# Attention and soft mixture of experts on one core: value rows in interleaved key order, a fourth value tile, and another opening

## The chip, the cores and the metric

The kernel runs on one core of a Trainium2 chip. The metric is device time in microseconds (us), the median of several runs. One more execution was profiled; everything below that is read from a trace comes from that execution.

## The reference

Queries attend in chunks of 32 to 8 memory keys, 16 keys to the left, the chunk's own 32 and 8 to the right (64 keys). The result x, 3072 rows of 512, goes through a soft mixture of eight experts.

```python
for c in range(nc):                      # 24 chunks of 32
    q_c = q[:, :, c_start:c_end]
    k_full = np.concatenate([mem_k, k[:, :, l_start:r_end]], axis=2)
    v_full = np.concatenate([mem_v, v[:, :, l_start:r_end]], axis=2)
    scores = scale * np.matmul(q_c, k_full.transpose(0, 1, 3, 2))
    a = softmax(scores)
    out[:, :, c_start:c_end] = np.matmul(a, v_full)
...
logits = x @ phi                         # 512 x 32
slot_input = softmax(logits, 0).T @ x    # 32 slots, 4 of each expert
h = np.maximum(slot_input[e] @ w1[e], 0.0); slot_out[e] = h @ w2[e]
return softmax(logits, 1) @ slot_out
```

## The kernel before

**Units.** The attention runs over 12 units (`NU`) of 256 queries, all 8 heads. In iteration i the loop turns the attention result of unit i-1 around (`transpose_x`), multiplies probabilities by values for unit i (`values`, tile `a`), makes scores for unit i+2 (`scores`, tile `s`) and transposes the probabilities of unit i+1 (`transpose_p`). VectorE subtracts the row maximum (`softmax`, tile `p`), ScalarE takes the exponent, VectorE sums and divides. After each pair of units the logits of the experts and a running `D` are brought up to date. Every engine keeps the order of the program text (`InOrder`); waits between engines come from the tiles' dependences.

**Tiles and loads.** All loads are issued on the sync engine's queue (SP), in program order, and a load waits there until its tile is free. Queries `q` (512 KB a unit) fill 128 partitions. Keys `k` come as two loads of 64 rows, for the two heads of a pair, onto every second partition. Values of a unit lie in two tiles: the even chunks' `e` and the odd chunks' `o`, each row 4 KB. `e` comes in two loads of 64 rows onto every second partition of 0 to 127 (from `vw`). The odd chunk's window shares its first 32 keys with the last 32 of `e`, so only 32 new rows a head are loaded (from `vx`), onto every second partition of 0 to 63, and `share_v` copies partitions 64 to 127 of `e` into `o` on GpSimd (POOL). `first_k` is a small POOL copy that puts the first chunk's keys beside the others; the scores wait for it. There are three buffers (`NB`) of `q`, `k` and of the value pair.

**Weights.** The expert weights are 64 pieces of 512 KB, 32 of `w1` and then 32 of `w2`. `load_w(upto)` issues pieces up to a count. The first 15 go to slabs of their own (`NW`); the count grows by 1.5 a unit (`WRATE`) through unit 7 and is then `usable[...]`, which adds the buffers of `k`, `q`, `v` and `x` as their last unit is done, 36 slabs in all. Later pieces take the slab of the piece 36 before. `hT` and other late tiles lie in a value pair that is no longer needed.

**Opening.** Tiles whose other head's half must be zero are cleared once: `k` by VectorE and POOL, the `e` tiles by ScalarE (three copies), the lower half of the `o` tiles by VectorE and POOL. Then follow the loads of units 0 to 2, with `first_k` and `share_v` between them in POOL's order.

After the attention the slot inputs are formed, four steps of two experts each run (tile `h`), then `w2` in two column blocks (tile `so`), each followed by `combine`, which writes half of the output.

Of the kernel before, what the change touches and what calls it, by code (L numbers as in the profile page):

```python
# [10 lines left out]
F32 = mybir.dt.float32  # L11
# [4 lines left out]
P = 128  # L16
# [27 lines left out]
NEG = -1.0e30  # L44
PIECE = 1024
NB = 3
NW = 15
W0 = 1
WRATE = 1.5
WLAST = 8  # L50
WARM0 = 8
WARM1 = 3
# [18 lines left out]
def tile_attn_softmoe(  # L71
# [2 lines left out]
    qT: bass.AP,  # L74
    kT: list,
    vw: bass.AP,
    vx: bass.AP,
    phi: bass.AP,
    w1: bass.AP,
    w2: bass.AP,  # L80
# [7 lines left out]

    q_t = [cp.tile([P, NPAIR, U], F32, tag=f"q{i}", name=f"q{i}") for i in range(NB)]
    k_t = [cp.tile([P, 2, KW], F32, tag=f"k{i}", name=f"k{i}") for i in range(NB)]  # L90
    v_t = [[cp.tile([P, 2, VW], F32, tag=f"v{i}{o}", name=f"v{i}{o}") for o in range(2)] for i in range(NB)]
    x_t = [cp.tile([P, 4, DM], F32, tag=f"x{i}", name=f"x{i}") for i in range(2)]
    w_slab = [cp.tile([P, PIECE], F32, tag=f"w{i}", name=f"w{i}") for i in range(NW)]
    lT = cp.tile([P, NG, P], F32, tag="lT", name="lT")
    late = [v_t[(NU - NB) % NB][o].rearrange("p a n -> p (a n)") for o in range(2)]
    hT = late[0].rearrange("p (e f s) -> p e f s", e=E, s=NSLOT)
    c_sb = late[1][:, 0:4 * NG * NSLOT].rearrange("p (u s) -> p u s", s=NSLOT)
    cst = [late[1][:, 4 * NG * NSLOT + P * G:4 * NG * NSLOT + P * G + P] for G in range(NG)]
# [16 lines left out]
    def load_q(u):  # L115
        sp.dma_start(q_t[u % NB], qT[u])
# [24 lines left out]
        pool.tensor_copy(out=kx[:, :, :, lo:CHUNK], in_=own[:, :, :, 0:CHUNK - lo])  # L141

    def load_v(u):
        e, o = v_t[u % NB]
        for h in range(2):
            sp.dma_start(e[h:P:2, h], vw[u, 64 * h:64 * h + 64])
        for h in range(2):
            sp.dma_start(o[h:P // 2:2, h], vx[u, CHUNK * h:CHUNK * h + CHUNK])

    def share_v(u):  # L150
        e, o = v_t[u % NB]
        pool.tensor_copy(out=o[P // 2:P], in_=e[P // 2:P])

    slabs = list(w_slab)
    freed = []
    for d in range(NB):
        u = NU - NB + d
        flat = k_t[u % NB].rearrange("p a n -> p (a n)")
        freed += [(2 * u - 3, flat[:, 0:PIECE]), (2 * u - 3, flat[:, PIECE:2 * PIECE])]
        freed += [(2 * u - 3, q_t[u % NB].rearrange("p g n -> p (g n)"))]  # L160
        if d:
            freed += [(2 * u, v_t[u % NB][o][:, a]) for o in range(2) for a in range(2)]
    flat_x = [t.rearrange("p u n -> p (u n)") for t in x_t]
    last = (NG - 1) % 2
    freed += [(2 * NU, flat_x[1 - last][:, 0:PIECE]), (2 * NU, flat_x[1 - last][:, PIECE:2 * PIECE])]
# [22 lines left out]
    pool.memset(k_t[0][:, 1], 0.0)  # L190
    make_identity(nc, ident)
    load_q(0)
    load_k(0)
    dve.memset(v_t[0][1][0:P // 2], 0.0)
    dve.memset(k_t[1][:, 0], 0.0)
    pool.memset(k_t[1][:, 1], 0.0)
    for u in range(NB):
        e = v_t[u][0].rearrange("p h n -> p (h n)")
        act.copy(out=e, in_=warm[:, 0:1].broadcast_to([P, 2 * VW]))
    load_k(1)  # L200
    load_q(1)
    load_v(0)
    first_k(0)
    dve.memset(v_t[1][1][0:P // 2], 0.0)
    share_v(0)
    load_v(1)
    sp.dma_start(phi_sb, phi.rearrange("(kc p) s -> p kc s", p=P))
    first_k(1)
    dve.memset(k_t[2][:, 0], 0.0)
    pool.memset(k_t[2][:, 1], 0.0)  # L210
    load_k(2)
    load_q(2)
    share_v(1)
    pool.memset(v_t[2][1][0:P // 2], 0.0)
    load_v(2)
    first_k(2)
    load_w(W0)
    w_ps = row(P, "warm_ps")

# [40 lines left out]
    def softmax(u, tiles):  # L260
        mx = wk.tile([P, 16, 1], F32, tag="mx", name=f"mx{u}")
        p = pexp[u] = wk.tile([P, 8, 4 * CHUNK], F32, tag="p", name=f"p{u}")
        step = NSUB // len(tiles)
        for a, t in enumerate(tiles):
            if u % UPB == 0 and a == 0:
                dve.memset(t[0:32, 0, :, :, 0:LEFT], NEG)
            if u % UPB == UPB - 1 and a == len(tiles) - 1:
                dve.memset(t[96:128, step - 1, :, :, CHUNK - RIGHT:CHUNK], NEG)
            m = mx[:, 8 * step * a:8 * step * (a + 1)]
            dve.tensor_reduce(out=m[:, :, 0], in_=t.rearrange("p s g h n -> p (s g h) n"), axis=AX.X, op=ALU.max)  # L270
            for h in range(2):
                dve.tensor_tensor(
                    out=p[:, 4 * step * a:4 * step * (a + 1)].rearrange("p m (n h) -> p h m n", h=2)[:, h],
                    in0=t.rearrange("p s g h n -> p h (s g) n")[:, h],
                    in1=m.rearrange("p (m h) o -> p h m o", h=2)[:, h].broadcast_to([P, 4 * step, 2 * CHUNK]),
                    op=ALU.subtract,
                )

# [25 lines left out]
    def values(u, pt):  # L304
        a_ps = banks(f"a{u}", "A").rearrange("p s (g h d) -> p s g h d", g=NPAIR, h=2)
        for s in range(NSUB):
            for g in range(NPAIR):
                for j in range(4):
                    v = v_t[u % NB][j % 2].rearrange("p h (i g d) -> p h i g d", g=NPAIR, d=D)
# [97 lines left out]
    for i in range(NU):  # L407
        G = (i - 2) // 2 if i >= 2 else None
        first = i % 2 == 0
        if i >= 1:  # L410
            transpose_x(i - 1)
        if i + 1 < NU:
            exponent(i + 1)
        if G is not None and not first:
            dispatch_t(G)
        a_ps = values(i, pt)
        if G is not None and first:
            l_ps = logits(G)
        if G is not None and not first:
            dispatch(G)  # L420
        normalize(i, a_ps)
        if i + 3 < NU:
            load_v(i + 3)
        load_w(W0 + int(WRATE * (i + 0.5)) if i < WLAST else usable[2 * i])
        if G is not None and first:
            dispatch_max(G, l_ps)
            dispatch_exp(G, l_ps)
        if G is not None and not first:
            dispatch_z(G)
            dispatch_sum(G)  # L430
# [184 lines left out]
def _layouts(inputs):  # L615
# [52 lines left out]
```

## Time and profile before

| | |
|---|---|
| median of 3 runs | 191.42 us (190.03 to 193.74) |
| the profiled execution | 187.95 us |
| its span, first to last instruction | 186.2 us |
| PE busy | 146.5 us (79%) |
| DVE busy | 101.2 us (54%) |
| ACT busy | 62.7 us (34%) |
| POOL busy | 36.3 us (19%) |
| bytes moved by DMA | 63.12 MB, mean 339 GB/s |

PE is TensorE, DVE VectorE, ACT ScalarE, POOL GpSimd, SP the sync engine whose queue issues the loads. Times in rows are in us from the start of the span. A share of busy time is an average over stages with different limits, so it names no bound by itself. The DMA share is the mean busy share of the core's 16 DMA engines; a transfer that takes longer than it should counts as busy too, so the share is read together with the GB/s beside it.

### The profile page before, as it was taken

The numbers are of one execution on the slowest core, as the hardware profiler recorded it, in microseconds if no ns is written. First come the engines' busy times: TensorE is split into PE (matmuls) and PEld (weight loads), VectorE is DVE, ScalarE is ACT, GpSimd is POOL, SyncE is SP. The second block draws the span as 40 slices with busy tenths as digits, with TensorE's granted clock in tenths as the row PEclk, the third lists the DMA queues.
The fourth block names the chain that finished last, engine by engine and source line by source line (L and its number), as shares of the span: only waits on it lengthen the run. The fifth ranks groups of instructions, "written<-read, shape, count | busy, mean of one in ns | idle before, by whom it ended". The sixth has DMA issues, their size and how long they took to land.

```text
span 186.2 us, 6128 instructions
## 1 busy us (share of the span) xinstructions
PE 146.5 (79%) x2649; PEld 108.2 (58%) x2649; DVE 101.2 (54%) x179; ACT 62.7 (34%) x122; POOL 36.3 (19%) x43
## 2 busy tenths in 40 slices
PE   4821996884999599789799588579999978867960
PEld 4711795773879488659778485264565635411530
DVE  6860399592679959597899934320560007100360
ACT  7620136231624806354273362200322006000350
POOL 6006901452223404050521800000000000000000
PEclk9996699999699999999999969957999999975576
DMA  5699789999999999999999999999999999999596
GB/s 164 217 276 219 229 258 383 340 392 284 386 293 314 323 338 383 260 362 258 334 303 263 388 402 415 410 407 408 408 410 406 409 406 408 408 411 420 213 407 249
DMA packets 18219, 63.12 MB, mean 339 GB/s; under 512 B 3088, under 2 KB 3088, under 8 KB 18192
## 3 DMA queue, kind: packets, MB, share of 16 engines
q1 hardware_dynamic: 18192, 62.73, 95.2%
q8 instruction: 21, 0.34, 0.8%
q14 instruction: 6, 0.05, 0.1%
HBM read 56.43 MB, written 6.29 MB: 337 GB/s over the span
## 4 chain that ended last, share of the span: by engine, by line
PE 46%; DMA 20%; DVE 16%; issue 7%; ACT 5%; SPq 1%; DVEq 0%; POOL 0%; ACTq 0%
PE s L65 10%; PE a L65 8%; PE h L65 7%; DMA w<-in_w_dram 5%; DMA k<-in_w_dram 5%; DMA v<-in_w_dram 5%; PE xt_ps L65 5%; PE pt_ps L65 4%; DMA v<-in_vw_dram 4%; DVE p L65 4%; DVE z L65 3%; DVE mx L65 3%; PE o L65 3%; ACT v L65 3%; DVE x L65 3%
## 5 line engine op out<-in xcount | busy, mean ns | idle before, releaser
L65 PE MATMUL s<-k,q 128*32 128x128 f32 x768 | 27.5, 292 | 13.9 <-POOL k L65 8.1
L65 PEld LDWEIGHTS s<-k,q 128*32 128x32 f32 x768 | 23.9, 118 | 18.3 <-issue 8.9
L65 POOL COPY v<-v 64x2048 f32<-64x2048 f32 x12 | 22.7, 1896 | 52.0 <-DMA v<-in_vw_dram 37.0
L65 PE MATMUL a<-v,pt 128*32 128x128 f32 x768 | 25.1, 277 | 4.6 <-issue 4.4
L65 ACT COPY pt<-pt_ps 128x512 f32<-128x512 f32 x24 | 13.1, 590 | 40.3 <-PE pt_ps L65 40.1
L65 PEld LDWEIGHTS a<-v,pt 128*32 128x32 f32 x768 | 20.8, 111 | 8.1 <-issue 6.4
L65 DVE TENSOR_REDUCE mx<-s 128x16 f32<-128x1024 f32 (+1 forms) x13 | 14.8, 1142 | 14.0 <-PE s L65 13.7
L65 DVE TENSOR_TENSOR x<-a,z 128x1024 f32<-128x1024 f32 x12 | 14.7, 1224 | 8.1 <-PE a L65 7.2
L65 PE MATMUL pt_ps<-ident,p 128*128 128x128 f32 x96 | 14.6, 298 | 2.5 <-issue 2.3
L65 DVE TENSOR_TENSOR p<-s,mx 128x512 f32<-128x512 f32 (+1 forms) x26 | 15.8, 656 | 0.5
L65 ACT ACTIVATE p<-p 128x1024 f32<-128x1024 f32 (+1 forms) x13 | 12.9, 994 | 7.0 <-DVE p L65 6.7
L65 PE MATMUL xt_ps<-ident,x 128*128 128x128 f32 x96 | 14.5, 298 | 0.9 <-DVE x L65 0.5
L65 ACT COPY xT<-xt_ps 128x512 f32<-128x512 f32 x24 | 13.4, 604 | 4.7 <-PE xt_ps L65 4.7
L65 DVE TENSOR_REDUCE z<-p 128x16 f32<-128x1024 f32 x12 | 14.6, 1214 | 0.0
L65 PEld LDWEIGHTS pt_ps<-ident,p 128*128 128x128 f32 x96 | 11.3, 150 | 5.2 <-issue 4.6
L65 PEld LDWEIGHTS xt_ps<-ident,x 128*128 128x128 f32 x96 | 12.4, 155 | 2.0 <-DVE x L65 1.4
L65 DVE COPY so_sb<-so 128x256 f32<-128x256 f32 x2 | 0.8, 424 | 19.7 <-PE so L65 19.7
L65 PE MATMUL o<-shl,v 32*128 32x256 f32 x96 | 9.8, 530 | 1.4 <-ACT shl L65 0.9
L65 PEld LDWEIGHTS o<-shl,v 32*128 32x128 f32 x96 | 6.5, 249 | 5.0 <-ACT shl L65 2.0
L65 POOL COPY k<-k 128x192 f32<-128x192 f32 (+2 forms) x20 | 5.8, 295 | 17.9 <-DMA k<-in_k_dram 17.2
L65 ACT COPY shl<-r 128x256 f32<-128x256 f32 x2 | 0.7, 373 | 23.5 <-PE r L65 23.5
L65 PE MATMUL h<-w,siT 128*32 128x256 f32 x120 | 8.5, 443 | 0.0
(95 smaller groups left out, 169.9 us busy)
## 6 DMA issues: line engine op xcount, KB each, us to landing
w<-in_w_dram SPq DMA_DIRECT2D x30, 512.0 KB, 9.8
q<-in_qT_dram SPq DMA_DIRECT2D x12, 512.0 KB, 7.2
v<-in_vw_dram SPq DMA_DIRECT2D x24, 256.0 KB, 7.9
k<-in_w_dram SPq DMA_DIRECT2D x12, 512.0 KB, 10.1
v<-in_w_dram SPq DMA_DIRECT2D x12, 512.0 KB, 10.2
v<-in_vx_dram SPq DMA_DIRECT2D x24, 128.0 KB, 7.6
q<-in_w_dram SPq DMA_DIRECT2D x6, 512.0 KB, 10.1
k<-in_k_dram SPq DMA_DIRECT2D x8, 296.0 KB, 7.0
```

The source lines that it names most:

```text
L65: return self.tc.keep_in_program_order(f(*args, **kwargs))
```

## The change

Positions in the score window are reordered. A probability column that stood for key 32b+j now lies at 2j+b, and the rows of the value tiles lie in the same order. In `o` the new rows then fall on every second row of a head, that is on partitions 4r and 4r+1 of all 128, and the shared rows on the others. `share_v` copies the whole of `e` into `o` (128 partitions), and `load_new` then overwrites the new rows from DRAM; it is issued at the top of iteration u-2 and waits for that copy. Units 0 and 1 load all 64 rows a head of `o` from DRAM instead (`load_odd`), with no copy. There is a fourth value pair (`NV`), so `e` is loaded four units ahead, not three; `NW` falls to 11 and `WRATE` to 1.25 to make room. The tiles cleared and the order of the opening differ. `phi` is laid out on the host so that each partition reads one run.

```diff
+NV = 4
+NDIRECT = 2
-NW = 15
+NW = 11
-WRATE = 1.5
+WRATE = 1.25
...
     def load_v(u):
-        e, o = v_t[u % NB]
+        e = v_t[u % NV][0]
         for h in range(2):
-            sp.dma_start(e[h:P:2, h], vw[u, 64 * h:64 * h + 64])
+            sp.dma_start(e[h:P:2, h], vw[u, 0, 64 * h:64 * h + 64])
+
+    def load_odd(u):
+        o = v_t[u % NV][1]
         for h in range(2):
-            sp.dma_start(o[h:P // 2:2, h], vx[u, CHUNK * h:CHUNK * h + CHUNK])
+            sp.dma_start(o[h:P:2, h], vw[u, 1, 64 * h:64 * h + 64])
 
     def share_v(u):
-        e, o = v_t[u % NB]
-        pool.tensor_copy(out=o[P // 2:P], in_=e[P // 2:P])
+        e, o = v_t[u % NV]
+        pool.tensor_copy(out=o, in_=e)
+
+    def load_new(u):
+        o = v_t[u % NV][1]
+        for h in range(2):
+            sp.dma_start(o[h:P:4, h], vw[u, 1, 64 * h:64 * h + 64:2])
...
-        if d:
-            freed += [(2 * u, v_t[u % NB][o][:, a]) for o in range(2) for a in range(2)]
+    for u in range(NU - NV + 1, NU):
+        freed += [(2 * u, v_t[u % NV][o][:, a]) for o in range(2) for a in range(2)]
...
+    dve.memset(warm, 0.0)
     dve.memset(k_t[0][:, 0], 0.0)
-    dve.memset(warm, 0.0)
     pool.memset(k_t[0][:, 1], 0.0)
+    for u in range(NDIRECT):
+        clear_v(act, u, 0)
+        clear_v(act, u, 1)
     make_identity(nc, ident)
+    dve.memset(k_t[1][:, 0], 0.0)
+    pool.memset(k_t[1][:, 1], 0.0)
     load_q(0)
     load_k(0)
-    dve.memset(v_t[0][1][0:P // 2], 0.0)
-    dve.memset(k_t[1][:, 0], 0.0)
-    pool.memset(k_t[1][:, 1], 0.0)
-    for u in range(NB):
-        e = v_t[u][0].rearrange("p h n -> p (h n)")
-        act.copy(out=e, in_=warm[:, 0:1].broadcast_to([P, 2 * VW]))
     load_k(1)
     load_q(1)
-    load_v(0)
-    first_k(0)
-    dve.memset(v_t[1][1][0:P // 2], 0.0)
-    share_v(0)
-    load_v(1)
-    sp.dma_start(phi_sb, phi.rearrange("(kc p) s -> p kc s", p=P))
-    first_k(1)
     dve.memset(k_t[2][:, 0], 0.0)
     pool.memset(k_t[2][:, 1], 0.0)
+    clear_v(dve, 2, 0)
+    first_k(0)
+    for u in range(NDIRECT):
+        load_v(u)
+        load_odd(u)
+    sp.dma_start(phi_sb, phi)
+    first_k(1)
+    clear_v(pool, 3, 0)
+    load_v(2)
     load_k(2)
     load_q(2)
-    share_v(1)
-    pool.memset(v_t[2][1][0:P // 2], 0.0)
-    load_v(2)
     first_k(2)
+    share_v(2)
+    load_v(3)
     load_w(W0)
...
                 dve.tensor_tensor(
-                    out=p[:, 4 * step * a:4 * step * (a + 1)].rearrange("p m (n h) -> p h m n", h=2)[:, h],
-                    in0=t.rearrange("p s g h n -> p h (s g) n")[:, h],
-                    in1=m.rearrange("p (m h) o -> p h m o", h=2)[:, h].broadcast_to([P, 4 * step, 2 * CHUNK]),
+                    out=p[:, 4 * step * a:4 * step * (a + 1)].rearrange("p m (j s h) -> p h m j s", s=2, h=2)[:, h],
+                    in0=t.rearrange("p s g h (b j) -> p h (s g) j b", b=2)[:, h],
+                    in1=m.rearrange("p (m h) o -> p h m o", h=2)[:, h].rearrange(
+                        "p m (o z) -> p m o z", z=1).broadcast_to([P, 4 * step, CHUNK, 2]),
                     op=ALU.subtract,
...
     for i in range(NU):
+        if NDIRECT <= i + 2 < NU:
+            load_new(i + 2)
...
         normalize(i, a_ps)
-        if i + 3 < NU:
-            load_v(i + 3)
+        if i + NV < NU:
+            load_v(i + NV)
...
         if i + 3 < NU:
             first_k(i + 3)
-        if i + 2 < NU:
-            share_v(i + 2)
+            share_v(i + 3)
```

## Rows read from the trace of the kernel before

**Rows 1.** Page, 40 slices of 4.66 us: DMA share in tenths, then GB/s.

```profile
DMA  5699789999999999999999999999999999999596
GB/s 164 217 276 219 229 258 383 340 392 284 386 293 314 323 338 383 260 362 258 334 303 263 388 402 415 410 407 408 408 410 406 409 406 408 408 411 420 213 407 249
```

**Rows 2.** Two stretches: length, busy per engine, granted clock, DMA share, GB/s.

```profile
8.00:109.00 101.00, 80.12 (x1835) 69.16 (x1828) 74.62 (x119) 38.87 (x74) 33.00 (x34) 0.94 0.99 315
109.00:170.40 61.40, 53.25 (x726) 29.96 (x724) 15.97 (x46) 12.98 (x34) 0.00 (x0) 0.89 1.03 410
```

**Rows 3.** The same view of short stretches inside the attention.

```profile
30.00:35.00 5.00, 2.90 (x96) 2.36 (x86) 3.01 (x5) 1.06 (x1) 2.78 (x4) 1.00 1.02 419
35.00:37.00 2.00, 2.00 (x27) 1.73 (x16) 1.58 (x3) 1.09 (x3) 0.00 (x0) 1.00 1.07 249
...
50.50:53.50 3.00, 3.00 (x91) 2.25 (x82) 1.82 (x2) 0.00 (x0) 0.00 (x0) 1.00 1.03 231
...
84.00:87.00 3.00, 3.00 (x67) 2.80 (x56) 1.66 (x4) 0.98 (x3) 0.00 (x0) 1.00 1.00 215
```

**Rows 4.** Timeline of SP's queue: start, time, tile and source of the issued loads.

```profile
2.25 4.76 SPq L65 DMA_DIRECT2D k<-in_k_dram  x4
...
7.69 1.11 SPq L65 DMA_DIRECT2D v<-in_vw_dram  x2
8.84 1.23 SPq L65 DMA_DIRECT2D v<-in_vx_dram  x2
...
15.35 4.20 SPq L65 DMA_DIRECT2D k<-in_k_dram  x2
...
31.13 1.14 SPq L65 DMA_DIRECT2D v<-in_vx_dram  x2
```

**Rows 5.** Page, DMA issues: source, count, KB each, median us to landing.

```profile
v<-in_vx_dram SPq DMA_DIRECT2D x24, 128.0 KB, 7.6
```

**Rows 6.** Chain that ended last, in order of time: start, time, what.

```profile
10.75 6.88 DMA v<-in_vw_dram
...
17.68 0.24 POOL k L65
...
160.40 9.99 DMA v<-in_w_dram
```

**Rows 7.** Timeline of PE's matmuls: start, time, tile, count, idle before and its releaser.

```profile
17.96 3.64 PE L65 MATMUL s<-k,q 128*32 128x128 f32 x64 [7.44 <-POOL k L65]
...
23.21 2.01 PE L65 MATMUL a<-v,pt 128*32 128x128 f32 x62 [0.24 <-DMA q<-in_qT_dram]
...
48.74 2.34 PE L65 MATMUL a<-v,pt 128*32 128x128 f32 x64
...
65.19 1.39 PE L65 MATMUL a<-v,pt 128*32 128x128 f32 x41 [1.97 <-issue]
...
111.00 1.96 PE L65 MATMUL a<-v,pt 128*32 128x128 f32 x64
...
124.86 1.51 PE L65 MATMUL h<-w,siT 128*32 128x256 f32 x12
```

**Rows 8.** Timeline of POOL, columns as in the group before.

```profile
15.43 1.89 POOL L65 COPY v<-v 64x2048 f32<-64x2048 f32 x1 [8.60 <-DMA v<-in_vw_dram]
...
21.05 1.80 POOL L65 MEMSET v<- 64x2048 f32 x1
...
105.04 1.83 POOL L65 MEMSET v<- 128x2048 f32 x1
```

**Rows 9.** Groups of instructions by line and shape: busy us, mean ns of one.

```profile
L65 DVE TENSOR_TENSOR p<-s,mx 128x512 f32<-128x512 f32 x22 | 14.3, 699 | 0.4
...
L65 ACT COPY v<-warm 128x2048 f32<-128x2048 f32 x3 | 5.5, 1894 | 0.4 <-DVE warm L65 0.4
...
L65 DVE TENSOR_REDUCE stats<-l 128x1 f32<-128x128 f32 x6 | 1.7, 283 | 2.2 <-PE l L65 2.2
...
L65 DVE TENSOR_REDUCE nms<-nm_ps 32x32 f32<-32x128 f32 x1 | 0.3, 278 | 1.0 <-PE nm_ps L65 1.0
```

More of the change, by code (lines that the diff above doesn't have):

```diff
@@ L76, in tile_attn_softmoe @@
     vw: bass.AP,
-    vx: bass.AP,
     phi: bass.AP,
@@ L90, in tile_attn_softmoe @@
     k_t = [cp.tile([P, 2, KW], F32, tag=f"k{i}", name=f"k{i}") for i in range(NB)]
-    v_t = [[cp.tile([P, 2, VW], F32, tag=f"v{i}{o}", name=f"v{i}{o}") for o in range(2)] for i in range(NB)]
+    v_t = [[cp.tile([P, 2, VW], F32, tag=f"v{i}{o}", name=f"v{i}{o}") for o in range(2)] for i in range(NV)]
     x_t = [cp.tile([P, 4, DM], F32, tag=f"x{i}", name=f"x{i}") for i in range(2)]
@@ L94, in tile_attn_softmoe @@
     lT = cp.tile([P, NG, P], F32, tag="lT", name="lT")
-    late = [v_t[(NU - NB) % NB][o].rearrange("p a n -> p (a n)") for o in range(2)]
+    late = [v_t[(NU - NV) % NV][o].rearrange("p a n -> p (a n)") for o in range(2)]
     hT = late[0].rearrange("p (e f s) -> p e f s", e=E, s=NSLOT)
@@ L184, in load_w, with clear_v @@
                 sp.dma_start(s, w2[at[0], at[1], :, at[2]])
+    def clear_v(eng, u, o):
+        t = v_t[u][o].rearrange("p h n -> p (h n)")
+        if eng is act:
+            act.copy(out=t, in_=warm[:, 0:1].broadcast_to([P, 2 * VW]))
+        else:
+            eng.memset(t, 0.0)
+    dve.memset(warm, 0.0)
     dve.memset(k_t[0][:, 0], 0.0)
-    dve.memset(warm, 0.0)
     pool.memset(k_t[0][:, 1], 0.0)
+    for u in range(NDIRECT):
+        clear_v(act, u, 0)
+        clear_v(act, u, 1)
     make_identity(nc, ident)
+    dve.memset(k_t[1][:, 0], 0.0)
+    pool.memset(k_t[1][:, 1], 0.0)
     load_q(0)
     load_k(0)
-    dve.memset(v_t[0][1][0:P // 2], 0.0)
-    dve.memset(k_t[1][:, 0], 0.0)
-    pool.memset(k_t[1][:, 1], 0.0)
-    for u in range(NB):
-        e = v_t[u][0].rearrange("p h n -> p (h n)")
-        act.copy(out=e, in_=warm[:, 0:1].broadcast_to([P, 2 * VW]))
     load_k(1)
     load_q(1)
-    load_v(0)
-    first_k(0)
-    dve.memset(v_t[1][1][0:P // 2], 0.0)
-    share_v(0)
-    load_v(1)
-    sp.dma_start(phi_sb, phi.rearrange("(kc p) s -> p kc s", p=P))
-    first_k(1)
     dve.memset(k_t[2][:, 0], 0.0)
     pool.memset(k_t[2][:, 1], 0.0)
+    clear_v(dve, 2, 0)
[7 more added lines that the diff above has]
+    load_v(2)
     load_k(2)
     load_q(2)
-    share_v(1)
-    pool.memset(v_t[2][1][0:P // 2], 0.0)
-    load_v(2)
     first_k(2)
+    share_v(2)
+    load_v(3)
     load_w(W0)
@@ L308, in values @@
                 for j in range(4):
-                    v = v_t[u % NB][j % 2].rearrange("p h (i g d) -> p h i g d", g=NPAIR, d=D)
+                    v = v_t[u % NV][j % 2].rearrange("p h (i g d) -> p h i g d", g=NPAIR, d=D)
                     pe.matmul(
@@ L443, in tile_attn_softmoe @@
         load_w(W0 + int(WRATE * (i + 1)) if i < WLAST else usable[2 * i + 1])
-        if i == NU - NB + 1:
+        if i == NU - NV + 1:
             pool.memset(hT, 0.0)
@@ L643, in windows @@
         return w.transpose(0, 4, 2, 3, 5, 1, 6).reshape(NU, 2 * len(first), CP, NPAIR * D)
-    vw = windows(range(2 * CHUNK))
-    vx = windows(range(2 * CHUNK, STEP + HALO))
+    even = [CHUNK * (r % 2) + r // 2 for r in range(2 * CHUNK)]
+    odd = [CHUNK * (2 - r % 2) + r // 2 for r in range(2 * CHUNK)]
+    vw = np.stack([windows(even), windows(odd)], axis=1)
+    phi = inputs["moe_phi"].reshape(NKC, P, NSLOT).transpose(1, 0, 2)
     w2 = inputs["moe_w2"].reshape(E, NFC, P, NBLK, WB).transpose(3, 0, 2, 1, 4).reshape(NBLK, E, P, 2, PIECE)
-    return {"qT": qT, **kT, "vw": vw, "vx": vx, "phi": inputs["moe_phi"], "w1": inputs["moe_w1"], "w2": w2}
+    return {"qT": qT, **kT, "vw": vw, "phi": phi, "w1": inputs["moe_w1"], "w2": w2}
 def kernel(**inputs):
```

## The prediction

> **What bounds the kernel now.** I read the slices first [rows 1]. From the third slice to the 37th the DMA engines are 70 to over 90% busy, yet until about 100 us the GB/s lie between 219 and 392, and after that near 408. Two stretches put that in one number each [rows 2]: from 8 to 109 us share 0.99 at 315 GB/s, from 109 to 170.4 us share 1.03 at 410. Engines that are always busy and carry a quarter less must be taking longer over each transfer. Short stretches show that this is no even slowness [rows 3]: 419 GB/s in one, then 249, 231 and 215, share at or above 1.00 throughout. The half-speed phases last 2 to 3 us and come once a unit, some 3 to 4 us after the two `vx` loads are issued (31.13 in [rows 4], phase from 35). Those are the only loads confined to partitions 0 to 63. Where only loads over all 128 partitions are in flight, such as `q`, `k` and `vw`, the rate is that of the weights. That `vx` slows everything beside it is my inference; the trace names no cause.
>
> The chain ends in weights, the last landing at 170.4 [rows 6]; 15.8 us of output follow. So to 170.4 the bound is DMA. Two side bounds matter if DMA gets cheaper. PE needs 62.3 us from `values(3)` to `values(11)`, 7.78 a unit, six gaps of "issue" among them (one is 1.97) [rows 7]. And `h` starts 13.9 us after `values(11)`.
>
> In the opening the second scores start at 17.96 after PE idled 7.44 [rows 7], released by `first_k(1)` [rows 6]. That copy stood in POOL's order behind `share_v(0)`, which itself waited 8.60 for `vw` [rows 8].
>
> **The change part by part.** *New rows on every fourth partition.* The bytes of `vx` stay (two loads of 32 rows a unit), but they spread over all 128 partitions. At 410 instead of 315 GB/s the 31.8 MB moved from 8 to 109 us would take 77.6 us: up to 23.4 us are to be had, at least nothing if the slowness comes with loads of 32 rows and not with their place. I take nearly all, since 64-row and 128-row loads, both spread, run at 398 to 419.
>
> [...]
>
> *Direct odd tiles.* Units 0 and 1 load 64 rows a head, not 32: four times 128 KB more, 0.52 MB, 1.3 us at 410 GB/s. A `vx` load takes 7.6 us to land [rows 5], so the new rows, issued about 1.5 units ahead, have some 4 us to spare. `phi` (64 KB, 0.2 us) is hidden behind the first units.
>
> *Opening.* `first_k(1)` no longer stands behind a value copy. `k` of unit 1 is issued by 7.0 us [rows 4]; with the 6.9 us to landing of a `vw` load under traffic [rows 6] it is there by 13.9, and the earliest is 10.5, when PE would otherwise idle. So the second scores gain 4.1 to 7.4 us. I take 6.7, nearer the upper end, because `k` goes ahead of the value loads on the queue: `values(0)` at 16.5 in place of 23.2 [rows 7]. ScalarE clears four tiles rather than three, 1.9 us more [rows 9], before it has an exponent to do; hidden, and at most 1.9 us otherwise. `k` of unit 2 now stands behind 2.6 MB of value rows rather than 1.6, but SP no longer waits until 15.35 to issue it.
>
> *Copies.* `share_v` writes 128 partitions in place of 64. A memset of 64 partitions takes 1.80, of 128 takes 1.83 [rows 8], so the copy stays at 1.89. There are 10, not 12. It moves one unit earlier, as does its `e`.
>
> *The wait of `load_new`.* At the top of iteration i SP waits for `share_v(i+2)`. Behind it stand `e` of unit i+4, weights and `k` and `q` of unit i+5. By my count `e` lands near the middle of iteration i-1 and the copy ends about when SP gets there: 0 to 3 us of wait. Transfers already issued cover it: a `vw` load takes 6.9 us from issue to landing. Cost nothing; 3 us for each of ten units where the cover fails.
>
> *`p` in the new order.* VectorE now reads PSUM alternately 32 elements apart. The nearest rows: a maximum over 128 PSUM elements taken 32 apart is 278 ns (`nms`), over 128 in a row 283 (`stats`) [rows 9]. So 699 ns a subtraction stays, two a unit. Bounds: nothing, or the double, 1.4 us a unit.
>
> *Fewer slabs.* By the end of unit 7 11 pieces may be out, not 13; in unit 8 14 and 17, not 18 and 21; from unit 9 on the counts agree (21, 24, 28, 32). All inputs and 11 pieces are 29.2 MB; 1.5 MB are moved by 8 us [rows 1], the rest takes 67.5 us: done at 75.5. If units take 7.6 us, `values(8)` ends near 79, so DMA idles up to 4 us there.
>
> **The sum.** Bound by DMA: 58.5 MB are moved by 170.4 now (1.5, 31.8 and 25.2 [rows 1, 2]), 59.0 after. From 8 us 57.5 MB at 410 take 140.2 us: 148.2, with the idle 4 us 152. Bound by PE: I take 7.6 us a unit, between 7.78 and 6.9 (without the issue gaps, 7.2 us in all): `values(11)` at 16.5 + 11 x 7.6 = 100.1, `h` at 114.0. All 36 slabs are full by then, so the 28 last pieces of 0.524 MB follow at 1.28 us each, 35.8 us: 150. The two nearly meet; I take 151 for the last weight, 19.4 us earlier than 170.4. The output stays at 15.8: 166.8 us of span. The profiled execution of 187.95 has 1.75 us around its span, so 168.5 on its scale. It lies 3.5 us below the median of 191.42; taking 19.4 from that gives 172.
>
> **Rivals.**
> 1. *The attention doesn't keep up* (0.14). DMA is freed, but PE still takes 7.78 a unit and the opening gains only 4.1: `values(11)` at 104.7, `h` at 118.6, last weight at 154.5 or, with one more unit of delay from instruction gaps, 158: 175.5 to 179. For it: on PE the gaps of "issue" may not come from the slow phases.
> 2. *The slowness stays* (0.08): it belongs to 32-row loads. Then 0.52 MB more cost 1.7 us at 315 GB/s, and the opening gains what DMA idles there, at most 5.6 us by the shares of the first two slices and the fifth [rows 1], of which I take 3.5. Time 189.6. Against it: 64-row loads are not slow.
> 3. *SP's wait takes the place* (0.04), slower. If each `load_new` lets the transfers run dry, ten units pay. It decides at 19.4 / 10 = 1.9 us of idle DMA a unit; at the full 3 us the last weight lands at 181 and the time is 202.
> 4. *Strided reads of PSUM* (0.02), slower. At the double, VectorE, busy 74.6 of 101 us [rows 2], gets 1.4 us a unit more and the units take about 8.4: near 180. It is slower than before only when `values(11)` comes after 120, so at 9.4 us a unit and three times the 699 ns. Rows 9 speak against it.
>
> [...]
>
> **The numbers.** The forecast has 0.72 and by itself the range 166 to 176 (opening between its bounds, 7.0 to 7.78 us a unit, no idle or 4 us). With rival 1 it holds 0.86; I let the range run from 165 to 182, which takes in 4 us more on either bound. Two per cent, 3.8 us, is about what a measurement here can tell from no change. Faster: forecast and rival 1, 0.86, and 0.01 of rival 4. Same: rival 2, 0.08. Slower: 0.05.
>
> **What would show it.** In the profile after: stretches of a unit near 400 GB/s with no phase at half rate; second scores before 14 us; `values(0)` near 16.5, `values(11)` near 100; the copy at 1.89 us on 128 partitions, `p` at 0.70; the last weight near 151. Half-rate phases that go on would prove rival 2; idle DMA with SP at `load_new` rival 3; full rate and idle DMA with late `values` rival 1.

## The result, and the profile after

The changed kernel took 179.48 us, the median of four runs (176.96 to 184.07), where the kernel before took 190.72 (188.99 to 193.74). The ratio is 0.932 with a 95% interval of 0.917 to 0.946; it is taken over the fast runs of both alone, so it lies a little under that of the medians (0.941). Six further runs beside the experiments gave 181.56 (176.89 to 184.04). So the change is faster, by about 10 us, and inside the forecast range of 165 to 182. The forecast of 172 asked for 19.4 us of gain, where the four runs gave 11.2 and the six beside their own runs of before (190.07) gave 8.5. By itself it had the range 166 to 176, and the result is outside that. The stated range held because of the room left for rival 1. The profiled execution took 177.4 us, span 175.6.

The page's 40 slices of 4.39 us, DMA share in tenths and GB/s, against [rows 1]:

```profile
DMA  5999999999999999989995999998999999999995
GB/s 144 306 350 384 322 408 401 304 361 407 415 308 397 411 394 359 331 306 312 365 405 192 387 396 413 413 407 308 310 407 418 405 405 409 411 405 420 379 411 208
```

Two stretches of after (length, busy per engine, granted clock, DMA share, GB/s), against [rows 2]:

```profile
8.00:109.00 101.00, 85.24 (x1921) 73.04 (x1916) 78.85 (x120) 42.26 (x81) 27.02 (x30) 0.95 0.97 362
109.00:159.82 50.82, 43.93 (x630) 25.34 (x623) 13.95 (x43) 9.98 (x28) 0.00 (x0) 0.93 1.01 392
```

In the attention the rate rose from 315 to 362 GB/s at a slightly lower share. DMA is faster, and now stands idle at times; it did not reach the 410 on which the sum was built.

PE's matmuls in order of time (start, time, tile, count, idle before and its releaser), against [rows 7]. The `a` lines kept here are `values(0)`, `(1)`, `(3)` and `(11)`:

```profile
11.70 1.95 PE L67 MATMUL s<-k,q 128*32 128x128 f32 x64 [0.48 <-POOL k L67]
...
14.91 2.35 PE L67 MATMUL a<-v,pt 128*32 128x128 f32 x64 [0.24 <-ACT pt L67]
...
21.71 3.46 PE L67 MATMUL s<-k,q 128*32 128x128 f32 x64 [4.46 <-DMA q<-in_qT_dram]
...
27.01 2.02 PE L67 MATMUL a<-v,pt 128*32 128x128 f32 x64
...
41.46 1.95 PE L67 MATMUL a<-v,pt 128*32 128x128 f32 x64
...
103.64 1.96 PE L67 MATMUL a<-v,pt 128*32 128x128 f32 x64
...
117.50 5.08 PE L67 MATMUL h<-w,siT 128*32 128x256 f32 x64
```

The chain that ended last puts the last weight at 149.75 + 10.06 = 159.8 (before 170.4 [rows 6]); the tail is 175.6 - 159.8 = 15.8, unchanged.

Cutting both executions at the same points shows where the 10.6 us came from: `values(0)` 8.3 earlier; `values(0)` to `values(3)` 26.55 in place of 25.53, 1.0 given back; `values(3)` to `values(11)` 62.18 in place of 62.26, nothing; `values(11)` to `h` 13.86 both times; `h` to the last weight 42.3 in place of 45.5, 3.2. The same cuts as stretches, first of before (`values(3)` to `values(11)`, to `h`, to the last weight):

```profile
48.74:111.00 62.26, 54.60 (x1253) 46.82 (x1252) 50.01 (x80) 28.20 (x57) 18.08 (x18) 0.97 1.00 325
111.00:124.86 13.86, 10.04 (x135) 6.89 (x135) 4.76 (x14) 3.09 (x10) 0.00 (x0) 0.87 1.03 411
124.86:170.40 45.54, 41.21 (x583) 21.40 (x582) 11.21 (x32) 8.62 (x22) 0.00 (x0) 0.91 1.03 409
```

and of after, the last one cut in two at 126:

```profile
41.46:103.64 62.18, 54.33 (x1253) 46.48 (x1252) 54.77 (x82) 27.20 (x56) 16.25 (x18) 0.97 0.96 356
103.64:117.50 13.86, 10.04 (x135) 6.89 (x135) 4.86 (x15) 3.75 (x12) 0.00 (x0) 0.86 1.03 412
117.50:126.00 8.50, 8.50 (x124) 4.50 (x127) 2.43 (x8) 1.21 (x2) 0.00 (x0) 0.83 0.93 305
126.00:159.82 33.82, 30.15 (x465) 17.15 (x455) 8.76 (x25) 7.41 (x20) 0.00 (x0) 1.00 1.02 409
```

The first pair carries the lesson. Eight units take the same 62 us with DMA at 325 GB/s and share 1.00 as with 356 and 0.96. PE is busy 54 to 55 of the 62 either way. In neither stretch does PE wait for a load. The units were not waiting for DMA, although DMA was always busy in before. The profiled execution of before took 187.95, though, less than any of the four runs above, so this holds for the two executions compared; two other kernels with confined loads, below, took 66.5 and 68.5 us over the eight units.

### The profile page after: what moved, and what is told of

It reads as the page before. It is cut to its first block, busy times and chain, and to the rows that moved or that the text cites. A ratio compares the mean times of both kernels' runs of the same rounds, so it can differ in the third digit from the quotient of the medians.

```text
span 175.6 us, 6120 instructions
## 1 busy us (share of the span) xinstructions
PE 141.5 (81%) x2649; PEld 107.3 (61%) x2649; DVE 102.9 (59%) x178; ACT 63.6 (36%) x123; POOL 31.7 (18%) x41
## 4 chain that ended last, share of the span: by engine, by line
PE 56%; DVE 13%; DMA 13%; ACT 6%; issue 6%; SPq 2%; DVEq 0%; ACTq 0%
PE s L67 11%; PE a L67 10%; PE h L67 9%; DMA v<-in_w_dram 6%; PE o L67 5%; PE so L67 4%; PE xt_ps L67 4%; PE pt_ps L67 4%; DMA v<-in_vw_dram 4%; DMA q<-in_qT_dram 3%; DVE z L67 3%; PE D_ps L67 3%; DVE p L67 2%; ACT v L67 2%; DVE mx L67 2%
## 5 line engine op out<-in xcount | busy, mean ns | idle before, releaser
L67 PE MATMUL s<-k,q 128*32 128x128 f32 x768 | 26.8, 290 | 12.8 <-issue 5.7
L67 PEld LDWEIGHTS s<-k,q 128*32 128x32 f32 x768 | 23.8, 117 | 16.5 <-issue 8.7
L67 PE MATMUL a<-v,pt 128*32 128x128 f32 x768 | 25.8, 286 | 1.6 <-issue 1.3
L67 POOL COPY v<-v 128x2048 f32<-128x2048 f32 x10 | 19.0, 1900 | 32.3 <-DMA v<-in_vw_dram 22.3
L67 PEld LDWEIGHTS a<-v,pt 128*32 128x32 f32 x768 | 21.9, 114 | 3.9 <-issue 2.1
L67 DVE TENSOR_TENSOR x<-a,z 128x1024 f32<-128x1024 f32 x12 | 14.7, 1224 | 4.5 <-PE a L67 3.7
L67 DVE TENSOR_TENSOR p<-s,mx 128x512 f32<-128x512 f32 (+1 forms) x26 | 15.8, 651 | 0.4
L67 PE MATMUL xt_ps<-ident,x 128*128 128x128 f32 x96 | 13.0, 276 | 3.3 <-DVE x L67 2.3
L67 DVE TENSOR_REDUCE z<-p 128x16 f32<-128x1024 f32 x12 | 14.7, 1222 | 0.0
L67 PEld LDWEIGHTS xt_ps<-ident,x 128*128 128x128 f32 x96 | 10.7, 141 | 5.1 <-DVE x L67 3.7
L67 PE MATMUL pt_ps<-ident,p 128*128 128x128 f32 x96 | 13.1, 280 | 0.0
L67 PEld LDWEIGHTS pt_ps<-ident,p 128*128 128x128 f32 x96 | 10.3, 140 | 2.4 <-issue 1.8
L67 ACT ACTIVATE d<-l,stats 128x128 f32<-128x128 f32 x6 | 2.2, 368 | 19.2 <-DVE lT L67 17.2
L67 ACT ACTIVATE hs<-h,rzd 128x512 f32<-128x512 f32 x4 | 2.8, 689 | 16.0 <-PE h L67 16.0
```

The lines of the kernel that those rows point to most:

```text
L67: return self.tc.keep_in_program_order(f(*args, **kwargs))
```

## The experiments

Single executions of one kernel differ by up to 4% here, so the experiments are read by their stages in the trace first and by their times second. Stages differ between executions too: two profiles of after, and two of kernels with the same program up to iteration 6, have `values(3)` at 41.5, 39.6, 44.5 and 40.5. A difference of less than 5 us at one such point, from one profile each, is weak evidence. Runs of before beside them had medians of 189.5 to 190.2.

### The loads alone: what do rows confined to partitions 0 to 63 do to others?

A kernel that leaves the attention and the experts out and has five phases of loads, each on fresh tiles: 32-row loads onto every fourth of 128 partitions; the same onto every second of 0 to 63; 64-row loads; confined 32-row loads mixed with whole weight pieces; spread ones mixed with the pieces.

```diff
+    phase("aq", ["quarter"] * 32)
+    phase("bl", ["lower"] * 32)
+    phase("ch", ["half"] * 16)
+    phase("dl", ["lower", "lower", "full"] * 8)
+    phase("eq", ["quarter", "quarter", "full"] * 8)
```

> Loads alone, in five groups one after the other, with no attention and no experts behind them (the outputs are only zeros): 32 loads of 32 rows on every fourth partition; 32 loads of 32 rows on every second partition of 0 to 63; 16 loads of 64 rows on every second partition; two loads of the lower form to one of 128 rows; two of the spread form to one of 128 rows. If the place is the cause, the second group runs at about half the rate of the first and the fourth is slower than the fifth. If loads of 32 rows are slow in themselves, the first two groups are alike and both well below the third.

One stretch inside each phase but the third (columns: length, busy of VectorE and POOL, granted clock, DMA share, GB/s):

```profile
12.00:31.00 19.00, 0.74 (x5) 0.00 (x0) 1.00 0.67 205
43.00:62.00 19.00, 0.69 (x4) 0.00 (x0) 1.00 0.69 204
...
99.00:117.00 18.00, 0.13 (x1) 0.00 (x0) 1.00 1.01 258
135.00:149.00 14.00, 0.00 (x0) 0.00 (x0) 1.00 0.97 346
```

The first two phases tell nothing apart: DMA idles a third of the time in both, and a load of 131 KB every 0.64 us gives 205 GB/s, so the limit lay ahead of the DMA engines: SP issued the 32 loads of the first phase in 20.29 us. In the mixed phases the place decides: the same bytes beside the same pieces move at 258 GB/s when confined and at 346 when spread. The pieces, spread themselves, are slowed too; their median time from issue to landing is the last number of the first two lines, that of the 32-row loads in the last two:

```profile
dl<-in_w_dram SPq DMA_DIRECT2D x8, 512.0 KB, 8.3
eq<-in_w_dram SPq DMA_DIRECT2D x8, 512.0 KB, 6.2
dl<-in_vw_dram SPq DMA_DIRECT2D x16, 128.0 KB, 7.3
eq<-in_vw_dram SPq DMA_DIRECT2D x16, 128.0 KB, 5.2
```

That is the step that the prediction could only infer.

### The place alone undone in the changed kernel

```diff
     def load_new(u):
-            sp.dma_start(o[h:P:4, h], vw[u, 1, 64 * h:64 * h + 64:2])
+            sp.dma_start(o[h:P // 2:2, h], vw[u, 1, 64 * h:64 * h + CHUNK])
```

with the order of `p` and of the rows as before; everything else stays.

> The changed kernel with one thing undone: natural key order, so that the new rows go to every second partition of 0 to 63 again; fourth tile, opening, load order and the copy of 128 partitions stay. If the place is the cause, a phase near 230 GB/s comes back in each unit, the stretch from 8 to 99 us falls from 358 to some 320 GB/s, the last weight lands near 168 and the time is 184 to 190. If the place doesn't matter, the time stays at 177 to 181.

186.55 us (185.41 to 188.04). One slow phase and the stretch from 8 to 99 us, then a slow place of after and the same stretch of it:

```profile
42.00:45.00 3.00, 3.00 (x16) 3.00 (x15) 2.97 (x4) 1.69 (x3) 1.65 (x2) 0.50 1.03 265
...
8.00:99.00 91.00, 76.33 (x1680) 65.46 (x1676) 63.26 (x103) 35.77 (x66) 26.90 (x30) 0.91 1.02 327
```

```profile
49.00:52.50 3.50, 3.50 (x118) 3.33 (x119) 3.29 (x7) 2.46 (x4) 0.19 (x2) 1.00 0.99 289
...
8.00:99.00 91.00, 76.48 (x1766) 66.87 (x1762) 72.38 (x108) 37.78 (x71) 27.02 (x30) 0.94 0.97 358
```

The slow phases are back, and the time with them. Stretches of 3 us, taken every 1.5 us from 30 us to `values(11)`, show how many: of those at a DMA share of 0.97 or more, 14 of 52 lie under 270 GB/s here, 8 of 46 in before, and none of 30 in after. Rival 2, slowness that belongs to 32-row loads, falls as the main cause; a little of it may be left, since the slowest such stretch of after has 287 GB/s, and that of the kernel below without any 32-row loads 373. In the changed kernel the place is worth 5 to 7 us. In the profile the last weight lands 9.1 us later than in after: 4.0 of them stand at `values(3)`, 4.3 more come in the eight units (66.5 us), 0.8 behind `h`. PE waits for no load in these units; the longer time is made of gaps of "issue" (6.7 us there, 4.9 in after), one wait of 2.2 for ScalarE and some matmuls at the lower clock (granted clock 0.94, in after 0.97). Whether slow loads cause any of that was not shown, and the split is one of single profiles.

### The place alone put into the kernel before

Three value pairs and 15 slabs stay, the opening too; only the order of the keys, the copy of all 128 partitions and `load_new`, one unit ahead:

```diff
+        if i + 1 < NU:
+            load_new(i + 1)
...
-        pool.tensor_copy(out=o[P // 2:P], in_=e[P // 2:P])
+        pool.tensor_copy(out=o, in_=e)
```

> The kernel before with the new order of rows alone: three value pairs, 15 slabs and the old opening stay; the new rows are loaded at the top of the iteration before their use, after the copy of all 128 partitions. If the place is what pays, the half-rate phases go and most of the gain is here: 179 to 184 us. If the opening and the earlier issue pay, it stays at 187 to 191.

191.41 us (189.96 to 192.85), no gain: the first branch of the expectation missed, and the result is 0.4 us above the second (187 to 191). PE's wait ahead of `values(1)`, and the stretch from 8 to 99 us:

```profile
32.17 2.15 PE L65 MATMUL a<-v,pt 128*32 128x128 f32 x36 [5.07 <-DMA v<-in_vw_dram]
```

```profile
8.00:99.00 91.00, 75.07 (x1646) 65.34 (x1642) 64.01 (x99) 34.30 (x65) 29.15 (x33) 0.91 0.89 318
```

DMA idles (share 0.89) at the old 318 GB/s, and PE waits for value rows, of which the new ones have to come after the copy in this program; similar waits of 0.9 to 3.6 us follow in later units. So the fourth pair and the issue two units ahead, which this run takes out together, are no extras. They keep the placement from turning into a wait.

### The opening alone put into the kernel before

```diff
     first_k(0)
+    first_k(1)
...
-    first_k(1)
```

> The kernel before with one POOL instruction moved: the key copies of unit 1 go ahead of the value copy of unit 0, so the second scores should start near 12 instead of 17.96. If DMA is the bound to the last weight, starting PE earlier brings little: 188 to 191 us. If the opening is what pays in the change, it brings 4 to 7 us: 183 to 187.

188.51 us (187.99 to 190.58), beside 189.53 for before. The second scores start at 12.84 in place of 17.96. `values(0)` and `values(3)`:

```profile
17.41 2.05 PE L65 MATMUL a<-v,pt 128*32 128x128 f32 x62 [0.24 <-ACT pt L65]
...
47.17 1.96 PE L65 MATMUL a<-v,pt 128*32 128x128 f32 x64
```

5.8 us earlier at `values(0)`, 1.6 at `values(3)` (before 48.74 [rows 7]). Most of the opening's gain is gone within three units; that the bytes for these units come slowly is the likely reason, not a shown one. The eight units then took 68.5 us in place of 62.3. PE waits for no load there; the difference is gaps of "issue", 15.3 us in place of 7.2.

### Three single edits beside a second set of runs of the changed kernel

> The changed kernel as it is, run beside the three kernels that take one thing out of it. Its first execution took 177.4 us with the last weight at 159.82, values(11) at 103.64, and 4.46 us of PE idle before the third scores. Theory: the gain that was forecast and did not come sits in three stalls of the PE chain (q of unit 2 late, VectorE held at 83 us, the weights after h), so the time falls again to 176 to 181 us, and the three kernels beside it move by the stalls that they take out.

181.56 us (176.89 to 184.04); its profiled execution has `values(3)` at 39.64, `values(11)` at 102.60 and the last weight at 159.1.

**`k` and `q` of unit 2 ahead of the value rows of unit 1:**

```diff
     load_v(0)
     load_odd(0)
+    load_k(2)
+    load_q(2)
     load_v(1)
     load_odd(1)
```

> The changed kernel with load_k(2) and load_q(2) issued ahead of load_v(1) and load_odd(1); nothing else. Theory (the early units are bound by PE's chain of waits, and q of unit 2 is late because 2.6 MB of value rows stand ahead of it): the third scores start near 17.5 to 18.5 in place of 21.71, the 4.46 us of PE idle go, values(1) comes near 23 to 24 in place of 27.01, and the last weight 2 to 4 us earlier: time 174 to 177 where the changed kernel itself takes 177 to 179. Rival (DMA has too many bytes to move in any case): values(1) earlier, values(11) and the last weight within 1 us of before, as with the opening alone put into the kernel before.

179.86 us (178.72 to 184.28): no difference from the 181.56 beside it. PE, third scores, fourth scores and `values(2)`:

```profile
17.82 1.95 PE L67 MATMUL s<-k,q 128*32 128x128 f32 x64
...
28.31 3.64 PE L67 MATMUL s<-k,q 128*32 128x128 f32 x64 [3.46 <-DMA q<-in_qT_dram]
...
34.37 1.95 PE L67 MATMUL a<-v,pt 128*32 128x128 f32 x64
```

The wait of 4.46 us is gone and one of 3.46 stands a unit later; `values(1)` comes 5.4 us earlier (21.60), `values(2)` 1.8 later than in after (32.60). So another order only moved the wait; a limit by the bytes that have to come in, up to about `values(2)`, would fit this and the DMA share of 0.99 to 1.01 in after from 8 to 33 us, but is not shown. The theory that the late `q` of unit 2 alone cost those microseconds falls.

**The clearing of `hT` moved to the end of the loop:**

```diff
-        if i == NU - NV + 1:
+        if i == NU - 1:
             pool.memset(hT, 0.0)
```

It was meant to part POOL's last copy from the memset, since in after VectorE's small `z` stood 2.76 us beside the two. POOL, then VectorE of after:

```profile
82.11 1.91 POOL L67 COPY v<-v 128x2048 f32<-128x2048 f32 x1 [4.63 <-DMA v<-in_vw_dram]
83.95 1.80 POOL L67 MEMSET v<- 128x2048 f32 x1
```

```profile
83.03 2.76 DVE L67 TENSOR_SCALAR z<-z 128x16 f32<-128x16 f32 x1
```

> The changed kernel with the clearing of hT on POOL moved from iteration 9 to iteration 11; nothing else. Theory (POOL's copy followed at once by its memset holds VectorE's z for 2.76 us, PE idles 1.60 and runs values(9) at the lower clock): z at about 83 us back at 0.2 us, values(11) 2 to 3 us earlier, time 1 to 3 us lower. Rival (the copy alone holds VectorE, or DMA bounds): z stays over 1 us there, or values(11) moves by under 1 us, and the time doesn't move.

181.93 us (179.63 to 183.24), no difference, and the edit did not do what it was for: POOL has nothing else to do between, so in program order the memset still follows the copy (85.59 and 87.45, as in after), and `z` took 1.70 us. It answers nothing.

**All odd tiles whole from DRAM, no copies:**

```diff
-NDIRECT = 2
+NDIRECT = 12
...
         if i + NV < NU:
             load_v(i + NV)
+            load_odd(i + NV)
...
-            share_v(i + 3)
```

> The changed kernel with the odd tiles of all 12 units loaded whole from DRAM, so that no POOL copy and no load_new is left; 10 units load 256 KB more each, 2.6 MB in all. Theory (bound by PE's chain and SP's waits, DMA has slack): 2.6 MB at 393 GB/s are 6.7 us of DMA against 18 us of idle share in the stretch from 8 to 99 and about 5 us of VectorE stalls beside POOL copies gone; the time lies within 3 us of the changed kernel's. Rival (bound by DMA): 5 to 7 us slower.

180.24 us (177.91 to 182.23), no difference from 181.56. The stretch from 8 to 99 us, then the 12 `z` of this kernel and those of after (groups by line: busy us, mean ns of one):

```profile
8.00:99.00 91.00, 75.14 (x1740) 64.25 (x1732) 66.97 (x107) 36.66 (x69) 10.09 (x21) 0.96 1.00 386
```

```profile
L67 DVE TENSOR_SCALAR z<-z 128x16 f32<-128x16 f32 x12 | 3.6, 302 | 0.4
```

```profile
L67 DVE TENSOR_SCALAR z<-z 128x16 f32<-128x16 f32 x12 | 7.2, 601 | 0.4
```

2.6 MB more went through at 386 GB/s, and the 12 `z` took 3.6 us less; neither moved the end by an amount that can be told. DMA had room for the bytes, as the theory said, though the share of 0.97 in after leaves 2.7 us of the stretch idle, not the 18 that it counted.

### Four slabs more, two slabs fewer

After these runs my theory was that DMA idles because 11 slabs are full until `values(9)`. Two kernels tested it. **Three pairs and 15 slabs, all odd tiles direct:**

```diff
-NV = 4
-NDIRECT = 2
-NW = 11
+NV = 3
+NDIRECT = 12
+NW = 15
-WRATE = 1.25
+WRATE = 1.5
```

> The odd tiles of all 12 units whole from DRAM as in the run with all of them direct, but with three value pairs, not four, since no copy has to come ahead of a load any more; the four slabs that this frees go to the weights (15 slabs and 1.5 pieces a unit, as in the kernel before). Theory (the changed kernel's DMA idles in the attention because 11 slabs are full until values(9), and after h it then has 28 pieces and a refill to bring): with four slabs more, the stretch from 8 to 99 us carries 395 to 405 GB/s in place of 358, the slabs are full before h starts, and the last weight lands at 150 to 156 in place of 159.82, although 2.6 MB more are moved: time 170 to 175. Rival (the end is set by values(11) and by what follows h, whatever lies in the slabs, or the third pair comes free too late): within 2 us of the run with all of them direct, 178 to 182.

182.98 us (180.89 to 186.34), 1 us above the rival's range. The theory fell: the stretch from 8 to 99 us carried 372 GB/s, not 395 to 405, `h` starts at 122.03, and the chain has the last weight at 164.5:

```profile
154.45 10.08 DMA v<-in_w_dram
```

164.5 is again 42.5 us after `h`. Four slabs more ahead of unit 9, with a value pair fewer, bought nothing. The last table has this distance for every run.

**9 slabs in place of 11:**

```diff
-NW = 11
+NW = 9
```

> The changed kernel with 9 slabs of its own in place of 11; nothing else. Theory (the end is set by how many pieces are in by the time that h starts): two pieces more come after h, and the last weight is 2 x 1.28 = 2.6 us later or somewhat more: 180 to 182 where the changed kernel takes 177.4. Rival (slabs are not short; the stretch before h has slack for them): no change.

189.46 us (187.82 to 194.99), far more than expected, and most of it from a side effect of the edit. The count of pieces still grew to 11 by the end of unit 7, so the 10th and 11th went to the `k` buffer of unit 9 around the scores of that unit. The 10th stands ahead of these scores in the program, which then read weights where half of the keys had been and wait until the piece has landed; the 11th waits on SP until they are done. SP's queue, and those scores on PE:

```profile
78.96 9.27 SPq L67 DMA_DIRECT2D k<-in_w_dram  x2
```

```profile
84.17 3.64 PE L67 MATMUL s<-k,q 128*32 128x128 f32 x64 [5.56 <-issue]
```

PE stood 5.56 us and took 3.64 us for these scores, where the next took 1.93 (mean granted clock 0.66 from 80 to 90 us), and all loads behind the two pieces stood 9.27 us on the queue; `values(11)` came at 112.74, 9.1 later than in after. The distance that the experiment was about is still readable. `h` starts at 126.60, and the chain has the last weight landing at 161.31 + 10.09 = 171.4:

```profile
161.31 10.09 DMA v<-in_w_dram
```

That is 44.8 us after `h`, 2.5 more than in after. Two more pieces of 1.28 us that have to wait for a slab would give 2.6; the kernels with 36 slabs lie between 41.7 and 43.1, so the agreement is no closer than that.

### The weights out of the attention

```diff
-WRATE = 1.25
+WRATE = 0.0
...
-        load_w(W0 + int(WRATE * (i + 0.5)) if i < WLAST else usable[2 * i])
+        load_w(W0 + int(WRATE * (i + 0.5)) if i < WLAST else W0)
```

> The changed kernel with one piece of the weights before the attention and all others after its last unit; the time is long, near 186 to 190 us, since 63 pieces of 1.28 us follow values(11), and only the units' pace is of use. Question: is the pace of the units set by PE's own work or by the weights' traffic beside it? Theory (PE's own work): values(3) to values(11) take 58 to 62 us as with the traffic (62.2), PE busy near 54 of them; the gaps of issue shrink at most. Rival (DMA traffic slows the units' own loads or instructions): the gaps of issue vanish and the stretch falls under 58 us, near PE's busy time.

185.63 us, as long as expected. Only its stretch from `values(3)` to `values(11)` counts:

```profile
40.17:101.61 61.44, 55.31 (x1253) 47.16 (x1252) 49.92 (x82) 27.38 (x56) 15.46 (x16) 0.94 0.83 291
```

61.4 us with DMA idle a sixth of the time, against 62.2 in after and 62.3 in before. The gaps of "issue" did not go either (6.7 us ahead of scores, against 5.7 in after). In this kernel the pace of the units is PE's own work and these gaps; it is one execution.

### The old opening in the changed kernel

Three `e` tiles cleared, values of unit 0 first, `first_k(1)` behind `share_v(0)`, and units 0 and 1 made by copy and `load_new` as all others; place, four pairs and 11 slabs stay.

```diff
     load_v(0)
     first_k(0)
+    share_v(0)
+    load_v(1)
...
     first_k(1)
...
+    load_new(0)
     load_k(2)
     load_q(2)
```

> The changed kernel with an opening in the order of the kernel before: three e tiles cleared by ScalarE, values of unit 0 ahead of the first scores' copies, first_k(1) behind share_v(0) on POOL, and the odd tiles of units 0 and 1 made by a copy and load_new as those of all other units (0.5 MB less to move). The new place, the fourth tile and the 11 slabs stay. In every run so far with 36 slabs but one the last weight landed 41.7 to 43.1 us after the start of h, and h starts 13.9 us or a little more after values(11), so the time follows values(11). Theory A (once the new rows lie on all partitions, the first units are limited by the bytes that have to come in, so a later start is mostly made up by unit 3): values(0) at 20 to 24, values(3) at 42 to 45 where the changed kernel has 41.5, values(11) within 4 us of 103.6 to 104, time 178 to 182. Rival B (the opening's gain is carried through): values(0) near 23, values(3) near 48 to 49 as before, values(11) near 110, time 184 to 187.

182.97 us (180.92 to 185.76): theory A on `values(3)` and `values(11)` (106.99), 1 us above its range in time. `values(0)` and `values(3)`:

```profile
19.29 2.05 PE L67 MATMUL a<-v,pt 128*32 128x128 f32 x64 [0.20 <-ACT pt L67]
...
43.05 1.95 PE L67 MATMUL a<-v,pt 128*32 128x128 f32 x64
```

4.4 us later than after at `values(0)`, 1.6 at `values(3)`. Most of the early gain belongs to the place with the fourth pair: `values(3)` is at 48.74 with neither, 47.17 with the opening alone, 43.05 with place and fourth pair, 41.46 with both, and 45.44 with opening and fourth pair but the old place. By the medians the opening adds 1.4 to 3.5 us of the whole (182.97 against 181.56 and 179.48, from different sets of runs); so little can't be told for certain beside such a spread.

### All runs cut at the same points

Worked out from the start of the `a` and `h` lines and the last weight of each profiled execution, in us:

| kernel | `values(3)` | `values(3)` to `(11)` | `h` to last weight |
|---|---|---|---|
| before | 48.7 | 62.3 | 45.5 |
| before, opening alone | 47.2 | 68.5 | 42.3 |
| before, place alone | 48.6 | 68.0 | 42.3 |
| after | 41.5 | 62.2 | 42.3 |
| after, second profile | 39.6 | 63.0 | 41.7 |
| after, old place | 45.4 | 66.5 | 43.1 |
| after, old opening | 43.1 | 63.9 | 42.5 |
| after, `k` and `q` of unit 2 first | 42.6 | 65.8 | 42.7 |
| after, late clearing | 44.5 | 64.6 | 42.7 |
| after, all direct | 44.3 | 62.5 | 42.1 |
| all direct, 15 slabs | 44.0 | 64.1 | 42.5 |
| after, 9 slabs (34 in all) | 40.5 | 72.3 | 44.8 |
| after, weights late | 40.2 | 61.4 | 51.4 |

The last column has the regularity that the prediction lacked. In every kernel with 36 slabs but before and the one with its weights held back, the last weight lands 41.7 to 43.1 us after `h`, however busy DMA was ahead of it; with 34 slabs it is 44.8. The end follows `h`, and `h` follows PE: it starts 13.9 us or a little more after `values(11)`.

## Why the prediction was right, and where it was wrong

**Right.** The direction, and the inference on the place: the half-rate phases came with rows confined to half of the partitions (258 GB/s in the mix of the loads alone, 346 with the rows spread), and they are gone. The second scores came at 11.70, 6.3 us earlier where the opening's step took 6.7, and `values(0)` at 14.91 (forecast 16.5). That the time fell into the stated range is no proof of the sum: its step on the bound and its step behind `h` were wrong, and the range took them in. The copy on 128 partitions takes 1900 ns, `p` in the new order 694 (699 before), SP waited for `load_new`'s copy 0.9 us in all, the bytes grew by 0.53 MB, the tail is 15.8: all terms as they stood or within 0.1, and rivals 2, 3 and 4 did not happen. Two groups (busy us, mean ns of one), and SP's wait for the copies (us in total, times, longest):

```profile
L67 POOL COPY v<-v 128x2048 f32<-128x2048 f32 x10 | 19.0, 1900 | 32.3 <-DMA v<-in_vw_dram 22.3 <-PE a L67 3.7 <-PE l L67 3.3
...
L67 DVE TENSOR_TENSOR p<-s,mx 128x512 f32<-128x512 f32 x22 | 14.3, 694 | 0.4
```

```profile
SPq L67 <- POOL v L67: 0.9, 2, 0.4
```

**Wrong: "So to 170.4 the bound is DMA".** A share near 1.00 over 160 us looked like the bound. By the runs it was one behind `h`, where the chain ends in a weight, and in the first units PE did wait for a load (4.46 us for `q` in after). Between `values(3)` and `values(11)` PE set the pace in the two executions compared. So of the 23.4 us of DMA time that the prediction took "nearly all" of, most was freed without a taker (undoing the place costs 5 to 7 us); from 8 to 109 us it became idle time and a rate of 362. The prediction had the side bound and even its rates: 7.6 us a unit was taken and (103.64 - 27.01) / 10 = 7.66 came. What it didn't see is that this bound, once the last term is right, held already.

**Wrong: the term after `h`.** The step read "All 36 slabs are full by then, so the 28 last pieces of 0.524 MB follow at 1.28 us each, 35.8 us". Measured were 42.3. By the stretches above, 8.5 us ran at 305 GB/s in place of 409, which costs 2.2 us; and 8.5 x 0.305 + 33.82 x 0.409 = 16.4 MB moved, not 14.7, so about three pieces issued earlier were still coming, 4.2 us. Together 6.4 of the 6.5 missing. SP's queue shows why the slabs were not full: the last four of the 36 are the `x` tiles, which come free only with the last units. Their pieces and the first that take a used slab, issued 1.1 us after `h` starts:

```profile
107.50 6.32 SPq L67 DMA_DIRECT2D x<-in_w_dram  x4
...
118.64 9.24 SPq L67 DMA_DIRECT2D w<-in_w_dram  x11
```

A piece into `x` takes 8.9 us to land (median), so some are on their way at 117.50. Both times hang on the end of the attention: in all ten kernels of 41.7 to 43.1 us the issue into `x` begins 8.2 to 10.0 us ahead of `h`, and that onto used slabs 1.1 us behind it. This is why the distance stays even where DMA had idled ahead of `h`. All direct (share 0.88 there) has 256 GB/s in the first 8.5 us, 3.2 us lost, and by the same sum 2.4 pieces still coming, 3.0 us: 6.2 of its 6.3. In before the issue into `x` began only 4.0 us ahead of `h` (SP, 120.84), and by the same sum 45.54 x 0.409 = 18.6 MB moved, so more was still on its way: 45.5.

**Wrong: the opening's cover.** `k` and `q` of unit 2 stood behind 2.6 MB of value rows, which the prediction named for `k`, and it let SP's earlier issue pay for it. SP did issue `q` earlier, at 15.77 in place of 19.61, but by 3.8 us only, where PE was ready for it 8.3 earlier. The chain shows it land at 21.58. PE waited 4.46 us for it and had a granted clock of 0.54 over the scores behind it. SP's line of before, then the chain of after:

```profile
19.61 0.58 SPq L65 DMA_DIRECT2D q<-in_qT_dram  x1
```

```profile
8.40 6.34 DMA v<-in_vw_dram
...
15.77 5.81 DMA q<-in_qT_dram
```

So `values(0)` to `values(1)` took 12.1 us, not 7.6. But the experiment that moved `q` shows that this was not one mis-sized wait: with another order a wait of 3.46 us stood one unit later, and the forecast pace was not kept there either.

In sum: `values(0)` 1.6 earlier than forecast, 4.5 lost by `values(1)`, 0.6 by the pace, 6.5 behind `h`, 1.0 that had been added by taking 151 rather than 150. -1.6 + 4.5 + 0.6 + 6.5 - 1.0 = 9.0 against 159.8 - 151 = 8.8.

Rival 1 (0.14) named the attention that doesn't keep up: `values(11)` at 104.7 and `h` at 118.6, where 103.64 and 117.50 came. It was nearer than the forecast, and its time of 175.5 missed only by the same term after `h`.

**Left open.** What ends PE's gaps of "issue" was not shown, and they weigh: 7.0 us in all in after, 11.3 with the late clearing, 15.3 in the eight units of the opening alone. They stand at fixed places of the program. Counted in matmuls, the gaps of a kernel lie some 126 apart or a multiple of that (in after at 598, 724, 977 and 1230, in before at 597, 975, 1228 and six more), and PE runs 2649, about 21 times 126. The page of after counts as many packets of instructions, 0.34 MB in all, so some 16 KB each:

```profile
q8 instruction: 21, 0.34, 0.8%
```

The two counts agree. That a gap is PE waiting for the next such packet is a guess, and what makes it long in one execution and not in another was not shown. Left open too are the shares of the fourth pair, of the issue two units ahead and of `phi`, which no run takes out by itself.

## What to carry to other kernels

A busy DMA is a bound only where someone waits for it: cut the trace at the same points in every run and see which distances move, before pricing the time that a faster transfer frees. Where buffers are refilled only as a late stage frees them, the end is the start of that stage plus the pieces behind it plus a restart; here that sum lay within 1.5 us in ten executions. Loads that fill only some rows of a tile were better spread over all partitions here (346 against 258 GB/s in the mix), but a load that must follow a copy also needs a buffer more and an issue early enough.

## What the hardware showed that was not expected

- 32-row loads confined to partitions 0 to 63 slowed whole weight pieces beside them too: 8.3 against 6.2 us from issue to landing, 258 against 346 GB/s in the mix, at a share near 1.00 both times. A DMA share near 1.00 so said nothing of the rate here.
- A VectorE operation on 128x16 elements (`z`, 0.18 us in the median of the 12 in after) once took 2.76 us, from inside a POOL copy (82.11 to 84.02) to the end of the POOL memset right behind it (85.75). In the second profile of after it took 2.50 us, with the late clearing 1.70, and each time it ended 0.03 to 0.04 us after such a memset. What held it was not shown. Without the copies the 12 `z` take 3.6 us, not 7.2.
- Two weight pieces issued onto a buffer around its last use held the load queue for 9.27 us, and from 80 to 90 us, with PE at work on the scores that the second one waited for (84.17 to 87.81), DMA moved 111 GB/s at a share of 0.38. `values(11)` came 9.1 us later, PE's wait of 5.56 among it: on a queue in program order the place of a load can cost more than its bytes (2 x 1.28 us).
